# The second MLP's first layer by seven products of quarters, its weights streamed

## The chip, the cores and the metric

One core of a Trainium2 chip runs the kernel, one launch of one program. The engines are TensorE (PE, matrix products; PEld is its weight load), VectorE (DVE), ScalarE (ACT), GpSimd (POOL) and SyncE (SP, which issues most transfers). Each engine works through its own list of instructions in order and waits at semaphores for the others. The metric is the device time of one execution in microseconds; the chip's trace gives each instruction's engine, start and duration.

## What is computed

Attention with decay over q, k, v of 4 batches, 8 heads, 768 positions and 64 columns; its output, 3072 tokens of 512 columns, goes through two MLPs. All values are float32.

```python
# per position t: state = gamma * state + k_t v_t^T ; y_t = scale * q_t state
# first MLP, 512 -> 1024 -> 512
h = x @ w_in;  solu = h * softmax(h);  ln = layernorm(solu) * g_ln;  x = ln @ w_out
# second MLP, 512 -> 2048 -> 512
h = x @ w_in;  g = h * np.cos(h);  out = g @ w_out
```

## The kernel before

Every large product is split: an operand a is kept as a high part (rounded to the type fp32r) and a low part (a minus its high part), and a product is the sum of three matrix products, high·high, low·high and high·low. A "piece" below is three such products of a 128x128 stationary tile with 512 columns, accumulated in a bank of PSUM.

The tokens are worked in 24 steps of 128 and then in 6 blocks of 512. The **first part** (to about 345 us) does attention and the first MLP: per step loads of q, k and v on SyncE, attention, first layer, norm; per block transposes (`transp`, L580, four products into one of two banks tr0 and tr1, from which ScalarE copies the high part and VectorE subtracts the low one) and the second layer (`mm2`), whose result goes to DRAM as y1d. Beside it the weights of the second MLP are unpacked: they are stored as pairs of words that `convert` (L471) puts together, and `keep` (L518) stores them in DRAM.

The **second part** does the second MLP by blocks. `load_y` (L646) loads a block of y1d and splits it into yh and yl. For each of 16 tiles j of 128 hidden columns, `up` (L672) makes the first layer, four pieces of 512 input columns in all (L681), into one of three banks h2, and then the cosine on two engines: ScalarE rounds h/2π to an integer ki (L685), VectorE subtracts ki times 2π in two steps and clamps (L687, L689, L691), ScalarE takes the sine (L693), VectorE multiplies with h (L695), ScalarE copies the high part gh (L697) and VectorE subtracts the low part gl (L699). `down` (L712) multiplies g of a tile with the output weights, four pieces into four banks acc0 to acc3 (L718), three tiles later than `up` (LAG = 3). The weights of this part stay in SBUF, split once into high and low parts by `load_kept` (L752).

A planner sets the order of all this. `P.add` records each operation with its engine, an estimated occupancy and the keys that it reads and writes; at the end `P.order` places the operations one after another by estimated start times and ranks, and emits every engine's list in that order. TensorE's operations may be taken from the next ten of the program's order.

Of the kernel before, what the change touches and what calls it, by code (L numbers as in the profile page):

```python
# [238 lines left out]
def body(ctx: ExitStack, tc: tile.TileContext, qkv, consts,  # L239
# [9 lines left out]
    p_w2a = ctx.enter_context(tc.tile_pool(name="w2a", bufs=1, side="right", reuse_waits="tile"))  # L249
# [221 lines left out]
    def convert(src, use, first=False):  # L471
# [34 lines left out]
    def load_w1(k, c):  # L506
        s = slice(c * 512, (c + 1) * 512)
        convert(w_in1[k * 128:(k + 1) * 128, c * 2048:(c + 1) * 2048],
                (w1h[:, k, s], w1l[:, k, s], ("w1h", k, c), ("w1l", k, c), None), first=(c + k == 0))
# [25 lines left out]
    def mm1(n, c, k, ms=(0, 1, 2)):  # L535
        h, hk = hbank(n, c)
        xh, xl = xhs[n % 2], xls[n % 2]
        s = slice(c * 512, (c + 1) * 512)

        def mm():  # L540
            for m in ms:
                a, w = ((xh, w1h), (xl, w1h), (xh, w1l))[m]
                nc.tensor.matmul(out=h, lhsT=a[:, k], rhs=w[:, k, s], start=(k + m == 0), stop=(k == KD - 1 and m == 2))  # L543
# [77 lines left out]


    def open_sb():
        att.close()
        p2["psh"] = ctx.enter_context(tc.tile_pool(name="psh", bufs=1, side="right", space=PSUM, reuse_waits="tile"))
# [372 lines left out]
```

## Time and profile before

| | us |
|---|---|
| median of 3 runs | 900.62 |
| lowest, highest | 896.74, 902.73 |
| profiled execution | 899.53 |
| its span | 897.7 |
| TensorE busy in it | 873.6 |
| VectorE busy | 571.2 |
| ScalarE busy | 421.5 |

The span runs from the first to the last event of the trace, and the execution's time is measured around it. Busy times of engines overlap. The trace was read as a page (shares of the span, the chain of work that ended last, groups of instructions, transfers) and by queries of stretches and single instructions. "Clock" is the granted clock of TensorE as a share of full speed.

### The profile page before, as it was taken

The numbers are of one execution on the slowest core, as the hardware profiler recorded it, in microseconds if no ns is written. First come the engines' busy times: TensorE is split into PE (matmuls) and PEld (weight loads), VectorE is DVE, ScalarE is ACT, GpSimd is POOL, SyncE is SP. The second block draws the span as 40 slices with busy tenths as digits, with TensorE's granted clock in tenths as the row PEclk, the third lists the DMA queues.
The fourth block names the chain that finished last, engine by engine and source line by source line (L and its number), as shares of the span: only waits on it lengthen the run. The fifth ranks groups of instructions, "written<-read, shape, count | busy, mean of one in ns | idle before, by whom it ended". The sixth has DMA issues, their size and how long they took to land.

```text
span 897.7 us, 14593 instructions
## 1 busy us (share of the span) xinstructions
PE 873.6 (97%) x5888; PEld 722.6 (80%) x5888; DVE 571.2 (64%) x1014; ACT 421.5 (47%) x701; POOL 45.9 (5%) x62
## 2 busy tenths in 40 slices
PE   5998999999999999999999999999999999999997
PEld 4777888888888878888888888888888888888886
DVE  4989858587473665476656565656655565557553
ACT  4688746466452464353343343334433443334332
POOL 2111201011010000000000000000000000000000
PEclk9998999999999999999999999999999999999999
DMA  9993688888520141220020002001200120011002
GB/s 265 295 336 96 189 276 269 296 254 297 161 81 32 50 139 65 82 106 1 24 71 0 1 24 71 0 1 46 49 1 0 48 47 1 1 48 24 1 0 48
DMA packets 38660, 85.17 MB, mean 95 GB/s; under 512 B 5440, under 2 KB 5440, under 8 KB 38592
## 3 DMA queue, kind: packets, MB, share of 16 engines
q1 hardware_dynamic: 38224, 83.24, 29.9%
q10 hardware_dynamic: 368, 0.99, 0.4%
q8 instruction: 46, 0.75, 0.3%
q14 instruction: 22, 0.18, 0.1%
HBM read 64.29 MB, written 19.92 MB: 94 GB/s over the span
## 4 chain that ended last, share of the span: by engine, by line
PE 90%; DMA 4%; DVE 2%; ACT 2%; issue 0%; SPq 0%; ACTq 0%
PE h L681 29%; PE acc L718 29%; PE y L612 12%; PE hA L543 11%; DMA in<-qkv_dram 4%; PE tr L612 2%; PE tr L588 2%; PE y L455 2%; PE sc L390 1%; DMA big<-w_in_dram 1%; ACT junk L321 1%; ACT u L321 0%; DVE in L324 0%; DVE u L332 0%; DVE sm L561 0%; PE S L398 0%
## 5 line engine op out<-in xcount | busy, mean ns | idle before, releaser
L693 ACT ACTIVATE r<-r,hp 128x512 f32<-128x512 f32 x96 | 69.5, 724 | 158.8 <-DVE r L691 158.8
L695 DVE TENSOR_TENSOR r<-r,h 128x512 f32<-128x512 f32 x96 | 66.0, 687 | 65.2 <-ACT r L693 65.2
L612 PE MATMUL y<-lt,o1h 128*128 128x512 f32 x320 | 105.3, 397 | 0.7 <-ACT ys L617 0.7
L687 DVE SCALAR_TENSOR_TENSOR r<-ki,h 128x512 f32<-128x512 int32 x96 | 65.9, 686 | 56.4 <-ACT ki L685 56.4
L699 DVE TENSOR_TENSOR gl<-r,gh 128x512 fp32r<-128x512 f32 x96 | 66.3, 690 | 46.3 <-ACT gh L697 46.3
L718 PE MATMUL acc<-o2u,gh 128*128 128x512 f32 x288 | 94.5, 389 | 0.0
L718 PE MATMUL acc<-o2h,gh 128*128 128x512 f32 x240 | 93.4, 389 | 0.0
L718 PE MATMUL acc<-o2h,gl 128*128 128x512 f32 x240 | 93.4, 389 | 0.0
L718 PE MATMUL acc<-o2l,gh 128*128 128x512 f32 x240 | 93.4, 389 | 0.0
L685 ACT ACTIVATE ki<-h 128x512 int32<-128x512 f32 x96 | 57.4, 598 | 75.1 <-PE h L681 75.1
L697 ACT ACTIVATE gh<-r 128x512 fp32r<-128x512 f32 x96 | 60.5, 630 | 53.0 <-DVE r L695 53.0
L543 PE MATMUL hA<-w1h,xh 128*128 128x512 f32 x176 | 72.2, 410 | 8.9 <-DVE u L332 6.9
L681 PE MATMUL h<-yh,w1h 128*128 128x512 f32 x192 | 74.7, 389 | 0.0
L681 PE MATMUL h<-yh,w1l 128*128 128x512 f32 x192 | 74.7, 389 | 0.0
L681 PE MATMUL h<-yl,w1h 128*128 128x512 f32 x192 | 74.7, 389 | 0.0
L612 PEld LDWEIGHTS y<-lt,o1h 128*128 128x128 f32 x320 | 60.0, 188 | 14.6 <-ACT ys L617 1.2
L543 PE MATMUL hA<-w1h,xl 128*128 128x512 f32 x176 | 69.0, 392 | 0.0
L543 PE MATMUL hA<-w1l,xh 128*128 128x512 f32 x176 | 68.6, 394 | 0.0
L689 DVE SCALAR_TENSOR_TENSOR r<-ki,r 128x512 f32<-128x512 int32 x96 | 66.4, 691 | 3.1
L718 PEld LDWEIGHTS acc<-o2u,gh 128*128 128x128 f32 x288 | 54.0, 188 | 11.2
L612 PE MATMUL y<-lt,o1l 128*128 128x512 f32 x160 | 62.3, 390 | 0.0
L681 PE MATMUL h<-yh,w2a 128*128 128x512 f32 x192 | 59.5, 391 | 0.0
(108 smaller groups left out, 1687.6 us busy)
## 6 DMA issues: line engine op xcount, KB each, us to landing
in<-qkv_dram SPq DMA_DIRECT2D x48, 256.0 KB, 5.1
in<-qkv_dram SPq DMA_DIRECT2D x95, 128.0 KB, 4.7
raw<-w_in_dram SPq DMA_DIRECT2D x16, 511.8 KB, 6.1
raw<-w_out_dram SPq DMA_DIRECT2D x16, 511.8 KB, 4.7
y1d<-ys SPq DMA_DIRECT2D x24, 256.0 KB, 2.5
x<-y1d SPq DMA_DIRECT2D x24, 256.0 KB, 3.1
out_dram<-o SPq DMA_DIRECT2D x48, 128.0 KB, 2.4
kept_out<-wt SPq DMA_DIRECT2D x16, 256.0 KB, 3.6
```

What stands on the lines that cost most here:

```text
L455: nc.tensor.matmul(out=p_y[64 * par:64 * par + 64, j], lhsT=W[par][:, j], rhs=X[par][:, j], start=True, stop=True)
L543: nc.tensor.matmul(out=h, lhsT=a[:, k], rhs=w[:, k, s], start=(k + m == 0), stop=(k == KD - 1 and m == 2))
L612: nc.tensor.matmul(out=y1(), lhsT=w[:, j, ds], rhs=lts[j][:, a], start=(j + m == 0), stop=(j == K1 - 1 and m == 2))
L681: nc.tensor.matmul(out=p2["h2"][b], lhsT=w2tile(c, lo)[:, k, cs], rhs=p2[a][:, k], start=(k + m == 0), stop=(k == KD - 1 and m == 2))
L685: P.add("ACT", 0.5, lambda: nc.scalar.activation(out=p2["ki"][s], in_=p2["h2"][b], func=AF.Identity, scale=INV2PI, bias=0.25), [("h2", b)] ...
L687: P.add("DVE", 0.61, lambda: V.scalar_tensor_tensor(out=p2["r"][s], in0=p2["ki"][s], scalar=-C1, in1=p2["h2"][b], op0=ALU.mult, op1=ALU.ad ...
L689: P.add("DVE", 0.61, lambda: V.scalar_tensor_tensor(out=p2["r"][s], in0=p2["ki"][s], scalar=-C2, in1=p2["r"][s], op0=ALU.mult, op1=ALU.add ...
L693: P.add("ACT", 0.62, lambda: nc.scalar.activation(out=p2["r"][s], in_=p2["r"][s], func=AF.Sin, bias=hp[:, 0:1]), (), [("r", s)])
L695: P.add("DVE", 0.6, lambda: V.tensor_tensor(out=p2["r"][s], in0=p2["r"][s], in1=p2["h2"][b], op=ALU.mult), [("h2", b)], [("r", s)])
L697: P.add("ACT", 0.54, lambda: nc.scalar.activation(out=p2["gh"][g], in_=p2["r"][s], func=AF.Copy), [("r", s)], [("gh", g)])
L699: P.add("DVE", 0.6, lambda: V.tensor_tensor(out=p2["gl"][g], in0=p2["r"][s], in1=p2["gh"][g].bitcast(F32), op=ALU.subtract), [("r", s), (" ...
L718: nc.tensor.matmul(out=p2["acc"][t], lhsT=p2[a][g][:, ts_], rhs=o2tile(j, lo), start=(j == 0 and m == 0), stop=(j == K2 - 1 and m == 2))
```

## The change

Blocks are taken in pairs, and the first layer of a pair is a product of 2x2 quarters: the halves of the 512 input columns, the two blocks of 512 tokens, and the halves of the 2048 hidden columns. Strassen's scheme (in Winograd's form) gives the four quarters of the result from seven products of sums and differences of quarters in place of eight products.

In the first part `prep_w`, `sum_w` and `split_w` make the seven combinations of weights, split them and store them in DRAM (wd, 28 stores of 512 KB), in place of the kept input weights. In the second part `load_w` fetches them tile by tile into a ring of 14 tiles (wr), in the space of the first MLP's weights; `load_x` makes the seven combinations of a pair's tokens. `up` does a "set": seven products of two pieces each into three banks (a: U0 or U3 in turn, b: U1, c: U2), in which products accumulate one on the other; between them ScalarE saves bank a to s, and VectorE adds s and a bank to get h. A set gives two hidden tiles (s and s+8) of both blocks. The even block's g is split and used at once by `down`; the odd block's g is stored to DRAM (gd) and fetched by `fetch_g` in a stretch of 16 `down` behind the pair's eight sets. `merge` puts 14 pieces of `up` and 8 of `down` in turns. All eight tiles of output weights are now loaded in one place (`load_o2`), and the transposes of the last block no longer have first-layer products between them.

```diff
+    def split_w(m, cc, kk, i):
+        n = spl[0] % 2
+        spl[0] += 1
+        st = stages[n]
+        f = wts[i].bitcast(F32).rearrange("p (j c) -> p j c", c=128)
+        act(st[:, :, 0], f, AF.Copy, [("wt", i)], [("st", n, 0)], 0.56)
+        tt(st[:, :, 1], f, st[:, :, 0].bitcast(F32), ALU.subtract, [("wt", i), ("st", n, 0)], [("st", n, 1)], port=True)
+        dma(lambda: nc.sync.dma_start(out=wd[cc][m][:, :, kk].rearrange("j p h c -> p j h c"), in_=st.bitcast(F32)), (512, 1024),
+            [("st", n, 0), ("st", n, 1)], [("wd", cc, m, kk)], occ=0.5)
...
+    def sum_w(o, a, b, op):
+        f = [wts[i].bitcast(F32) for i in (o, a, b)]
+        tt(f[0], f[1], f[2], op, [("wt", a), ("wt", b)], [("wt", o)], port=True)
...
+    def prep_w(cc, kk, step):
+        def piece(mh, kh, i):
+            k, c = kk + 2 * kh, cc + 2 * mh
+            convert(w_in2[k * 128:(k + 1) * 128, c * 2048:(c + 1) * 2048], i)
+        if step == 0:
+            piece(1, 0, 2)
+        if step == 1:
+            piece(1, 1, 3)
+            sum_w(4, 2, 3, ALU.add)
+            split_w(3, cc, kk, 3)
+            split_w(4, cc, kk, 4)
+        if step == 2:
+            piece(0, 0, 0)
+            sum_w(5, 4, 0, ALU.subtract)
+            sum_w(2, 0, 2, ALU.subtract)
+            split_w(0, cc, kk, 0)
+            split_w(5, cc, kk, 5)
+            split_w(6, cc, kk, 2)
+        if step == 3:
+            piece(0, 1, 1)
+            split_w(1, cc, kk, 1)
+            sum_w(1, 1, 5, ALU.subtract)
+            split_w(2, cc, kk, 1)
...
-    def load_y(n):
-        for k in range(KD):
-            b = k % 2
-            dma(lambda k=k, b=b: nc.sync.dma_start(out=x32s[b].rearrange("p a t -> p (a t)"), in_=y1d[n][:, k]), (128, 2048),
-                [("y1d", n, k)], [("x32", b)])
-            P.add("ACT", 0.54, lambda k=k, b=b: nc.scalar.activation(
-                out=p2["yh"][:, k], in_=x32s[b].rearrange("p a t -> p (a t)"), func=AF.Copy),
-                [("x32", b)], [("yh", k)], after=p2["sb_hook"])
-            P.add("DVE", 0.6, lambda k=k, b=b: nc.vector.tensor_tensor(
-                out=p2["yl"][:, k], in0=x32s[b].rearrange("p a t -> p (a t)"), in1=p2["yh"][:, k].bitcast(F32),
-                op=ALU.subtract), [("x32", b), ("yh", k)], [("yl", k)], port=True, after=p2["sb_hook"])
...
+        def part(kk):
+            def sub(o, a, b):
+                f, k = zip(*(half(q) for q in (o, a, b)))
+                tt(f[0], f[1], f[2], ALU.subtract, k[1:], k[:1], port=True)
+
+            def split(m, q):
+                f, k = half(q)
+                P.add("ACT", 0.54, lambda: nc.scalar.activation(out=p2["x"][m][0][:, kk], in_=f, func=AF.Copy),
+                      [k], [("x", m, 0, kk)], after=hook)
+                P.add("DVE", 0.6, lambda: nc.vector.tensor_tensor(
+                    out=p2["x"][m][1][:, kk], in0=f, in1=p2["x"][m][0][:, kk].bitcast(F32), op=ALU.subtract),
...
+            def get(q, n, k):
+                f, key = half(q)
+                dma(lambda: nc.sync.dma_start(out=f, in_=y1d[n][:, k]), (128, 2048), [("y1d", n, k)], [key])
+            get(0, 2 * p, kk)
+            get(1, 2 * p, kk + 2)
+            get(2, 2 * p + 1, kk)
+            get(3, 2 * p + 1, kk + 2)
+            split(0, 0)
+            split(1, 1)
+            sub(4, 2, 0)
+            split(4, 4)
+            sub(5, 3, 4)
+            split(5, 5)
+            sub(1, 1, 5)
+            split(3, 1)
+            sub(2, 3, 2)
+            split(6, 2)
+            split(2, 3)
+        part(0)
+        part(1)
...
+    def products(s):
+        return (0, 1, 5, 4, 6, 3, 2) if s < 7 else (0, 1, 5, 6, 3, 4, 2)
+
+    wn = [0]
+    slot = {}
+
+    def load_w(p, s):
+        for m in products(s):
+            n = wn[0] % NWR
+            wn[0] += 1
+            slot[p, s, m] = n
+            dma(lambda n=n, m=m: nc.sync.dma_start(out=p2["wr"][n].bitcast(F32), in_=wd[s // 4][m][s % 4]), (128, 2048),
+                [("wd", s // 4, m, kk) for kk in (0, 1)], [("wr", n)], after=p2["ring_hook"])
+
+    hn, rn = [0], [0]
...
+              [hk], [("r", r)], port=not bank)
+        if n % 2 == 0:
+            split_g(n, j, lambda: p2["r"][r], ("r", r), j % 2 * 2 + j // 8)
+        else:
+            d = dram.tile([128, 512], F32, name=f"gd{n}_{j}")
+            p2["gd", n, j] = d
+            dma(lambda: nc.sync.dma_start(out=d, in_=p2["r"][r]), (128, 2048), [("r", r)], [("gd", n, j)])
...
+    def fetch_g(n, j, i):
+        b = i % (16 - NWR)
+        dma(lambda: nc.sync.dma_start(out=p2["gs"][b], in_=p2["gd", n, j]), (128, 2048), [("gd", n, j)], [("gs", b)],
+            after=p2["ring_hook"])
+        split_g(n, j, lambda: p2["gs"][b], ("gs", b), i % 4 if i < 10 else 2 + i % 2)
...
+    def up(p, s):
...
+        sets = p * 8 + s
+        a, b, c = 3 * (sets % 2), 1, 2
+        bank = {0: a, 1: b, 4: c, 5: a, 3: a, 6: a, 2: c}
...
+        def save(i):
+            P.add("ACT", 0.5, lambda: nc.scalar.activation(out=p2["s"][i], in_=p2["U"][a], func=AF.Copy), [ka], [("s", i)],
+                  after=p2["cos_hook"])
...
+        def add(n, j, i, u):
+            k = hn[0] % 4
+            hn[0] += 1
+            P.add("DVE", 0.6, lambda: nc.vector.tensor_tensor(out=p2["h"][k], in0=p2["s"][i], in1=p2["U"][u], op=ALU.add),
+                  [("s", i), ("ub", u)], [("h", k)], after=p2["cos_hook"])
+            cosine(n, j, lambda: p2["h"][k], ("h", k))
...
+        def piece(m, kk):
+            u = bank[m]
+
+            def mm():
+                for q, (lo, xl) in enumerate(((0, 0), (1, 0), (0, 1))):
+                    nc.tensor.matmul(out=p2["U"][u], lhsT=p2["wr"][slot[p, s, m]][:, kk, lo], rhs=p2["x"][m][xl][:, kk],
+                                     start=(kk + q == 0 and m in (0, 1, 4)), stop=(kk == 1 and q == 2),
+                                     skip_group_check=True)
+            hook = (*p2["sb_hook"], *p2["ring_hook"], *(p2["wo_hook"] if u == 3 else ()))
+            P.add("PE", 0.68, mm, [("wr", slot[p, s, m]), ("x", m, 0, kk), ("x", m, 1, kk)], [("ub", u)], lat=0.93, after=hook)
+            if kk == 0:
+                return
+            if m == 0:
+                save(0)
+            if m == 1:
+                add(2 * p, s, 0, b)
+            if m == 5:
+                save(1)
+            if m == 6:
+                save(0)
+            if m == (6 if s < 7 else 4):
+                add(2 * p + 1, s + 8, 0, c)
+            if m == 3:
+                cosine(2 * p, s + 8, U(a), ka, True)
+            if m == 2:
+                add(2 * p + 1, s, 1, c)
+        return [lambda m=m, kk=kk: piece(m, kk) for m in products(s) for kk in range(2)]
...
+    p2["ring_hook"] = [P.add("HOOK", 0.0, open_ring, lat=0.0, after=P.using({"w1h", "w1l"}))]
+    load_x(0)
+    load_w(0, 0)
+    load_w(0, 1)
+    for j in range(K1):
+        transp(g, j)
+    p2["cos_hook"] = [P.add("HOOK", 0.0, open_cos, lat=0.0, after=P.using({"u", "x32"}))]
+    mm2(g, 0, None)
+    last = up(0, 0)
+    for d in range(1, 4):
+        mm2(g, d, d % 2)
+        for f in last[(d - 1) * 4:d * 4]:
+            f()
     p2["wo_hook"] = [P.add("HOOK", 0.0, open_wo, lat=0.0, after=P.using({"big", "o1h", "o1l", "xh", "xl", "junk", "ys", "hb"}))]
-    for q in range(2):
...
+    for s in range(4):
+        load_o2(s // 2 if s % 2 == 0 else 4 + s // 2)
+    for s in range(4):
+        load_o2(2 + s // 2 if s % 2 == 0 else 6 + s // 2)
+    for f in last[12:]:
+        f()
+    for p in range(NBLK // 2):
+        for s in range(1, 8):
+            if s < 7:
+                load_w(p, s + 1)
+            a, b = up(p, s), down(2 * p, s - 1, 0) + down(2 * p, s - 1, 1)
+            if s < 7:
+                merge(a, b)
+            else:
+                for f in a[:6] + b[:2] + a[6:8] + b[2:4] + a[8:] + b[4:]:
+                    f()
+        if p + 1 < NBLK // 2:
+            load_x(p + 1)
+            load_w(p + 1, 0)
+            load_w(p + 1, 1)
+        rest = down(2 * p, 7, 0) + down(2 * p, 7, 1)
+        for f in rest:
+            f()
+        for s in range(8):
+            for e in range(2):
+                fetch_g(2 * p + 1, s + 8 * e, 2 * s + e)
+                d = down(2 * p + 1, s, e)
+                if p + 1 < NBLK // 2 and s >= 6:
+                    i = 2 * (s - 6) + e
+                    if i == 0:
+                        nxt_up = up(p + 1, 0)
+                    merge(d, nxt_up[i * 4:i * 4 + 4])
+                else:
+                    for f in d:
+                        f()
```

Three places of the engines' lists. In VectorE's list a set, in the second part. Before, two hidden tiles (L687 and L689 subtract, L691 clamps, L695 multiplies, L699 is the low part):

```order
L695 TENSOR_TENSOR r0_3361<-r0_3361,h20_3354 128x512
L699 TENSOR_TENSOR gl2_3369<-r0_3361,gh2_3365 128x512
L687 SCALAR_TENSOR_TENSOR r1_3362<-ki1_3360,h21_3355 128x512
L689 SCALAR_TENSOR_TENSOR r1_3362<-ki1_3360,r1_3362 128x512
L691 TENSOR_SCALAR r1_3362<-r1_3362 128x512
L695 TENSOR_TENSOR r1_3362<-r1_3362,h21_3355 128x512
L699 TENSOR_TENSOR gl3_3370<-r1_3362,gh3_3366 128x512
```

Now the same operations are L771, L773, L775, L779 and L791, and L818 adds a saved bank and a bank; the first half of a set,

```order
L818 TENSOR_TENSOR hb_3871<-s_3872,U2_3514 128x512
L771 SCALAR_TENSOR_TENSOR ra_3873<-ki_3875,hb_3871 128x512
L773 SCALAR_TENSOR_TENSOR ra_3873<-ki_3875,ra_3873 128x512
L771 SCALAR_TENSOR_TENSOR rb_3874<-ki_3875,U3_4029 128x512
L775 TENSOR_SCALAR ra_3873<-ra_3873 128x512
L773 SCALAR_TENSOR_TENSOR rb_3874<-ki_3875,rb_3874 128x512
L818 TENSOR_TENSOR hb_3871<-s_3872,U2_3514 128x512
L775 TENSOR_SCALAR rb_3874<-rb_3874 128x512
L779 TENSOR_TENSOR ra_3873<-ra_3873,hb_3871 128x512
L771 SCALAR_TENSOR_TENSOR rb_3874<-ki_3875,hb_3871 128x512
L773 SCALAR_TENSOR_TENSOR rb_3874<-ki_3875,rb_3874 128x512
L779 TENSOR_TENSOR rb_3874<-rb_3874,U3_4029 128x512
```

and its second half, after which the next set begins:

```order
L818 TENSOR_TENSOR ha_3870<-s_3872,U1_3513 128x512
L775 TENSOR_SCALAR rb_3874<-rb_3874 128x512
L791 TENSOR_TENSOR gl3_3532<-rb_3874,gh1_3878 128x512
L771 SCALAR_TENSOR_TENSOR ra_3873<-ki_3875,ha_3870 128x512
L779 TENSOR_TENSOR rb_3874<-rb_3874,hb_3871 128x512
L773 SCALAR_TENSOR_TENSOR ra_3873<-ki_3875,ra_3873 128x512
L775 TENSOR_SCALAR ra_3873<-ra_3873 128x512
L779 TENSOR_TENSOR ra_3873<-ra_3873,ha_3870 128x512
L791 TENSOR_TENSOR gl0_3529<-ra_3873,gh_3876 128x512
L818 TENSOR_TENSOR ha_3870<-s_3872,U2_3514 128x512
```

Before, one chain stands behind the other; now four chains and three additions of a set interlace, and the last three operations follow each other's results.

TensorE's list, at the end of a hidden tile's first layer before (L681, then the second layer, L718):

```order
L681 MATMUL h21_3355<-yh_3357,w2h3_3869 128x512
L681 MATMUL h21_3355<-yh_3357,w2l3_3870 128x512
L681 MATMUL h21_3355<-yl_3358,w2h3_3869 128x512
L718 MATMUL acc0_3865<-o2h5_3875,gh3_3366 128x512
L718 MATMUL acc0_3865<-o2h5_3875,gl3_3370 128x512
L718 MATMUL acc0_3865<-o2l5_3876,gh3_3366 128x512
L718 MATMUL acc1_3866<-o2h5_3875,gh3_3366 128x512
```

Now the end of a set (L860 is the second layer, L827 the first; x6, x3, x2 are products 6, 3 and 2 of the seven):

```order
L860 MATMUL acc2_4027<-o2h6_4042,gh_3876 128x512
L860 MATMUL acc2_4027<-o2h6_4042,gl1_3530 128x512
L860 MATMUL acc2_4027<-o2l6_4043,gh_3876 128x512
L860 MATMUL acc3_4028<-o2h6_4042,gh_3876 128x512
L860 MATMUL acc3_4028<-o2h6_4042,gl1_3530 128x512
L860 MATMUL acc3_4028<-o2l6_4043,gh_3876 128x512
L827 MATMUL U3_4029<-x3h_3521,wr12_3702 128x512 x2
L827 MATMUL U3_4029<-x3l_3522,wr12_3702 128x512
L827 MATMUL U3_4029<-x3h_3521,wr12_3702 128x512 x2
L827 MATMUL U3_4029<-x3l_3522,wr12_3702 128x512
L827 MATMUL U2_3514<-x2h_3519,wr13_3703 128x512 x2
L827 MATMUL U2_3514<-x2l_3520,wr13_3703 128x512
```

Before, each tile had a bank of its own; now product 3 accumulates in bank U3, which product 6 finished some pieces earlier and which is saved in between, and product 2 follows at once in U2.

TensorE's list, at the transposes of the last block before (h21 is a bank of the second MLP's first layer):

```order
L681 MATMUL h21_3355<-yl_3358,w2a0_160 128x512
L588 MATMUL tr0_822<-ident_85,u6_100 128x128
L588 MATMUL tr0_822<-ident_85,u0_94 128x128
L588 MATMUL tr0_822<-ident_85,u1_95 128x128
L588 MATMUL tr0_822<-ident_85,u2_96 128x128
L588 MATMUL tr1_823<-ident_85,u6_100 128x128
```

Now (same tiles, new lines):

```order
L636 MATMUL tr1_897<-ident_82,u2_107 128x128
L636 MATMUL tr0_896<-ident_82,u6_111 128x128
L636 MATMUL tr0_896<-ident_82,u0_105 128x128
L636 MATMUL tr0_896<-ident_82,u1_106 128x128
L636 MATMUL tr0_896<-ident_82,u2_107 128x128
L636 MATMUL tr1_897<-ident_82,u6_111 128x128
```

Before, a pair of transposes stood behind a first-layer tile; now tr0 and tr1 come again right behind their first use, four transposes in a row.

## Rows read from the trace of the kernel before

**Rows 1.** The page, part 1: busy us, share of the span, instructions.
```profile
PE 873.6 (97%) x5888; PEld 722.6 (80%) x5888; DVE 571.2 (64%) x1014; ACT 421.5 (47%) x701; POOL 45.9 (5%) x62
```

**Rows 2.** The page, part 4: the chain that ended last, by engine.
```profile
PE 90%; DMA 4%; DVE 2%; ACT 2%; issue 0%; SPq 0%; ACTq 0%
```

**Rows 3.** The chain's pieces in order of time: start, us, what.
```profile
457.20 10.88 PE h L681 x48
```

**Rows 4.** Stretches: bounds, length, busy us (count) by engine, clock, DMA share, GB/s.
```profile
50.00:100.00 50.00, 44.98 (x605) 37.13 (x605) 47.84 (x96) 44.69 (x80) 10.33 (x10) 0.93 0.58 188
100.00:150.00 50.00, 50.00 (x428) 41.26 (x430) 34.72 (x74) 27.90 (x47) 6.76 (x9) 1.00 0.81 265
150.00:200.00 50.00, 50.00 (x564) 41.66 (x554) 35.96 (x75) 28.74 (x48) 5.55 (x7) 1.00 0.85 276
200.00:250.00 50.00, 50.00 (x490) 41.50 (x490) 31.98 (x69) 26.14 (x46) 6.49 (x8) 1.00 0.66 214
```

**Rows 5.** Timeline 600 to 612 us: start, us, engine, line, operation [idle before, releaser].
```profile
603.92 0.39 PE L718 MATMUL acc<-o2h,gh 128*128 128x512 f32 x1
...
604.18 0.60 ACT L685 ACTIVATE ki<-h 128x512 int32<-128x512 f32 x1 [0.79 <-PE h L681]
...
604.81 0.69 DVE L687 SCALAR_TENSOR_TENSOR r<-ki,h 128x512 f32<-128x512 int32 x1 [0.69 <-ACT ki L685]
...
605.53 0.69 DVE L689 SCALAR_TENSOR_TENSOR r<-ki,r 128x512 f32<-128x512 int32 x1
...
606.26 0.43 DVE L691 TENSOR_SCALAR r<-r 128x512 f32<-128x512 f32 x1
...
606.72 0.72 ACT L693 ACTIVATE r<-r,hp 128x512 f32<-128x512 f32 x1 [1.94 <-DVE r L691]
...
607.48 0.69 DVE L695 TENSOR_TENSOR r<-r,h 128x512 f32<-128x512 f32 x1 [0.79 <-ACT r L693]
...
608.20 0.63 ACT L697 ACTIVATE gh<-r 128x512 fp32r<-128x512 f32 x1 [0.76 <-DVE r L695]
...
608.87 0.69 DVE L699 TENSOR_TENSOR gl<-r,gh 128x512 fp32r<-128x512 f32 x1 [0.70 <-ACT gh L697]
```

**Rows 6.** Timeline of VectorE, 360 to 368 us, a dense stretch.
```profile
363.74 0.42 DVE L691 TENSOR_SCALAR r<-r 128x512 f32<-128x512 f32 x1
364.07 0.68 DVE L687 SCALAR_TENSOR_TENSOR r<-ki,h 128x512 f32<-128x512 int32 x1
364.79 0.69 DVE L689 SCALAR_TENSOR_TENSOR r<-ki,r 128x512 f32<-128x512 int32 x1
365.40 0.68 DVE L695 TENSOR_TENSOR r<-r,h 128x512 f32<-128x512 f32 x1
365.99 0.42 DVE L691 TENSOR_SCALAR r<-r 128x512 f32<-128x512 f32 x1
```

**Rows 7.** Groups by line and form: line, operation, count, busy us, mean ns, idle before.
```profile
L324 DVE TENSOR_TENSOR x<-y,mg 128x512 f32<-128x512 f32 x24 | 16.6, 690 | 0.5
...
L617 ACT ACTIVATE ys<-y 128x512 f32<-128x512 f32 x20 | 11.9, 596 | 38.4 <-PE y L612 26.9 <-DMA y1d<-ys 7.3 <-issue 3.1
...
L760 DVE TENSOR_TENSOR o2l<-raw,o2h 128x1024 fp32r<-128x1024 f32 x5 | 6.0, 1222 | 13.5 <-ACT o2h L759 13.5
...
L759 ACT ACTIVATE o2h<-raw 128x1024 fp32r<-128x1024 f32 x5 | 5.2, 1050 | 0.0
```

**Rows 8.** The page, part 6: transfers of 256 KB, us from issue to landing.
```profile
x<-y1d SPq DMA_DIRECT2D x24, 256.0 KB, 3.1
```

**Rows 9.** Stretches of 10 us, columns as in rows 4.
```profile
60.00:70.00 10.00, 5.53 (x111) 4.48 (x109) 9.85 (x24) 9.45 (x16) 2.59 (x3) 0.91 1.04 330
70.00:80.00 10.00, 9.45 (x40) 7.80 (x40) 9.26 (x15) 8.28 (x16) 1.42 (x1) 0.75 0.08 23
320.00:330.00 10.00, 9.26 (x41) 7.35 (x40) 5.59 (x12) 7.71 (x10) 0.55 (x1) 1.00 0.37 112
```

**Rows 10.** Timeline of TensorE, 320 to 324 us: a product behind a wait.
```profile
322.49 0.50 PE L612 MATMUL y<-lt,o1h 128*128 128x512 f32 x1 [0.74 <-ACT ys L617]
```

More of the change, by code (lines that the diff above doesn't have):

```diff
@@ L537, in mm1 @@
         xh, xl = xhs[n % 2], xls[n % 2]
-        s = slice(c * 512, (c + 1) * 512)
         def mm():
             for m in ms:
-                a, w = ((xh, w1h), (xl, w1h), (xh, w1l))[m]
-                nc.tensor.matmul(out=h, lhsT=a[:, k], rhs=w[:, k, s], start=(k + m == 0), stop=(k == KD - 1 and m == 2))
+                a, lo = ((xh, 0), (xl, 0), (xh, 1))[m]
+                nc.tensor.matmul(out=h, lhsT=a[:, k], rhs=w1[lo][k][c], start=(k + m == 0), stop=(k == KD - 1 and m == 2))
         r = [("xh", n % 2)]
@@ L703, in o2tile, with half @@
-    def o2tile(j, lo):
-        g = j // 2
-        if g < UBUF // 2:
-            return o2u[2 * g + lo][:, j % 2]
-        return p2["o2"][g][lo][:, j % 2]
-    def o2key(g, lo):
-        return [("u", 2 * g + lo, c) for c in (0, 1)] if g < UBUF // 2 else [("o2", g, lo)]
-    def down(n, j, tiles=range(4)):
-        g = p2["g", n, j]
-        for t in tiles:
-            def mm(t=t):
+    def half(q):
+        return raws[q // 2][:, (q % 2) * 512:(q % 2 + 1) * 512].bitcast(F32), ("raw", q // 2, q % 2)
@@ L755, in load_kept, with merge @@
         t = raws[n % NRAW].bitcast(F32).rearrange("p (e f) -> p e f", e=2)
-        rk = ("raw", n % NRAW)
-        d = kept[what]
-        dma(lambda: nc.sync.dma_start(out=t, in_=d), (128, 4096), [("kept",) + what + (k,) for k in (0, 1)], [rk])
-        P.add("ACT", 0.95, lambda: nc.scalar.activation(out=tile_of(0), in_=t, func=AF.Copy), [rk], hk, after=after)
-        P.add("DVE", 1.14, lambda: nc.vector.tensor_tensor(out=tile_of(1), in0=t, in1=tile_of(0).bitcast(F32),
-                                                           op=ALU.subtract), [rk] + hk, lk, port=True, after=after)
+        rk = [("raw", n % NRAW, h) for h in (0, 1)]
+        d = kept[g]
+        dma(lambda: nc.sync.dma_start(out=t, in_=d), (128, 4096), [("kept", g, k) for k in (0, 1)], rk)
+        P.add("ACT", 0.95, lambda: nc.scalar.activation(out=p2["o2"][g][0], in_=t, func=AF.Copy), rk, [("o2", g, 0)],
+              after=p2["wo_hook"])
+        P.add("DVE", 1.14, lambda: nc.vector.tensor_tensor(out=p2["o2"][g][1], in0=t, in1=p2["o2"][g][0].bitcast(F32),
+                                                           op=ALU.subtract), rk + [("o2", g, 0)], [("o2", g, 1)], port=True,
+              after=p2["wo_hook"])
+    def merge(a, b):
+        n, m = len(a), len(b)
+        i = j = 0
+        while i < n or j < m:
+            if j >= m or (i < n and i * m <= j * n):
+                a[i]()
+                i += 1
+            else:
+                b[j]()
+                j += 1
     loaded = [0]
@@ L805, in attend @@
         if n == ns - 1:
-            p2["sb_hook"] = [P.add("HOOK", 0.0, open_sb, lat=0.0, after=P.using({"in", "amg", "sc", "S", "y"}))]
+            p2["sb_hook"] = [P.add("HOOK", 0.0, open_sb, lat=0.0, after=P.using({"in", "amg", "sc", "S", "y", "wt", "st", "top"}))]
     def first(n, c):
```

199 lines of the change are left out of this document (78 added, 121 removed).

## The prediction

> **What bounds the kernel now.** I read the page's busy shares first: TensorE is busy for 873.6 of 897.7 us, VectorE for 64%, ScalarE for 47% [rows 1]. A share this high makes TensorE's work the first suspect, and the chain that ended last confirms it: 90% of it is TensorE, transfers and the other engines share the rest [rows 2]. The chain's pieces then tell at which rate that work runs: 48 products of the second MLP's first layer take 10.88 us [rows 3], so a product of 512 columns costs 10.88/48 = 0.2267 us and a piece of three 0.68 us. The stretches show where it is not so: from 50 to 100 us TensorE loses 5.0 us of 50, VectorE being busy for 47.84 there; from 100 us on it is busy throughout at clock 1.00, with VectorE at 32 to 36 of 50 [rows 4]. So a product that goes away in the second part is worth 0.2267 us, as long as VectorE, ScalarE and the banks keep up at the shorter pace. That is the question of this case, since the change pays for its products in VectorE, ScalarE and transfers.
>
> My sum is made against the profiled execution, 899.53 us (897.7 of span and 1.83 around it); the median of the runs is 900.62, 0.12% above.
>
> **Products removed.** Seven products of quarters in place of eight: the first layer goes from 1152 to 1008 products, the second stays at 1152, the rest of TensorE's list keeps its numbers. 144 x 0.2267 = 32.6 us less. Nothing covers TensorE there, so all of it counts if no new wait comes: 866.9 us.
>
> **A set of four hidden tiles.** A set is 14 pieces of the first layer with 8 pieces of the second between them: 22 x 0.68 = 14.96 us of TensorE. Its other side is VectorE: three additions of a saved bank to a bank, four cosine chains of four operations, two low parts, 17 long operations and 4 clamps (the order rows of VectorE). Two views price them. In the ordinary run of the kernel before, a chain shows each operation and each trip to ScalarE: 0.69 us an operation, 0.43 the clamp, and waits of 0.69, 0.79 and 0.70 us for ScalarE's three steps [rows 5]. In a dense stretch the operations start closer than they last: those at 364.79, 365.40 and 365.99 start 0.61 and 0.59 apart, one that needs the result just before it 0.72, and after a clamp the next starts 0.33 later [rows 6]. With the starts of the dense stretch, 17 x 0.60 + 4 x 0.34 = 11.6; the order leaves three trips to ScalarE uncovered (behind the addition of U2, and behind the last clamp and the last multiplication of the set), each the operation's time and the wait less the start already counted: 0.69 + 0.69 - 0.60, 0.43 + 0.79 - 0.34 and 0.69 + 0.70 - 0.60, together 2.45; four starts behind their own result add 0.12 each, 0.5. Sum 14.5 us, below 14.96: TensorE still sets the pace, with 0.5 us to spare. I take this value, because the rows with the short starts are VectorE's own under load. The other end has no overlap at all: 17 x 0.69 + 4 x 0.43 = 13.45, plus the waits of 0.69, 0.79 and 0.70, is 15.63 us.
>
> The Trainium skill ("VectorE: DVE Perf Modes", section "Terms") has a rule that speaks for that other end: each operation is followed by a flush, and the next can't issue until the pipe is empty. By it the sets would be paced by VectorE; the starts 0.6 us apart of operations that last 0.68 or 0.69 [rows 6] speak against it, and the measurement decides.
>
> **ScalarE.** A set has three saves, four first steps, four sines, two copies of high parts: 7 x 0.60 + 4 x 0.72 + 2 x 0.63 = 8.3 us of 14.96 [rows 5, 7]; free, apart from its place in the waits.
>
> **Waits for banks.** The tightest point of TensorE in a set is product 3: it starts at 18 x 0.68 = 12.24 us and overwrites nothing, but accumulates into the bank that must first be saved after product 6, which ends at 16 x 0.68 = 10.88. From the last piece to ScalarE's start the trace shows 0.26 us (603.92 to 604.18), a copy out of a bank takes 0.60 [rows 5, 7]: free at 11.74, 0.5 us early. Product 2 at 13.60 needs the addition of U2, of 0.69 us, behind that save: about 12.5, 1.1 us early. A queue on ScalarE of one operation eats the first margin now and then: between 0 and 18 x 0.3 = 5 us, I take 1.
>
> **Streaming.** A tight set fetches seven weight tiles and stores two tiles of g, 9 x 256 KB in 14.96 us, 158 GB/s; the trace moved 276 GB/s from 150 to 200 us [rows 4], and the ring holds two sets, so a transfer of 3.1 us [rows 8] has a set's time. Free; without that cover the price is the transfer, once per set. The fetches of the odd block have 5.44 us per round of two buffers against 3.1 + 0.60 + 0.69 = 4.4: free too.
>
> **The turn from the first part to the second.** Eight transposes used to have first-layer products of the second MLP between them; now four stand in a row over two banks (the order rows of the transposes). Each bank is copied (0.26 + 0.60) and subtracted (0.69) before it is free [rows 5, 7], so the third waits some 1.2 us and the fourth 0.2: +1.4. Afterwards pieces of the first MLP's second layer lie between.
>
> **The first sets.** Eight tiles of output weights are split there, 1.05 us on ScalarE and 1.22 on VectorE each [rows 7]; some of the eight were split in the same place before, beside a VectorE with more room. Against 0.5 us of room per set, 8 x 1.22 = 9.8 us has to be fitted into the looser first set: 0 to 5 us, I take 2.
>
> **Preparation in the first part.** 16 sums, and 28 splits for 4, are 40 more long operations on VectorE, 40 x 0.69 = 27.6 us [rows 7], mostly between 100 and 250 us, where it is busy for 34.72 + 35.96 + 31.98 = 102.7 of 150 [rows 4]; 130.3 is 87%. At 69% TensorE loses nothing, at 96% (50 to 100) 5 of 50, though cold start and loads share that blame. Between them lie 0 and about 10 us; no product waits for a prepared weight until the second part, so I take 2.5. The stores of prepared weights, 28 x 512 KB, stand in SyncE's order later than the loads that TensorE waits for; the transfer share of 0.81 to 0.85 [rows 4] is why I don't take 0.
>
> Sum: 866.9 + 1 + 1.4 + 2 + 2.5 = 873.8, **874 us**.
>
> **Rivals.**
> *VectorE paces the sets* (15.63 for 14.96): 18 tight sets (6 in each of 3 pairs) x 0.67 = 12 us, 886. For: three new additions and uncovered trips. Against: [rows 6]. Chance 0.14.
>
> *The preparation delays the first part* by its upper bound, 10 us instead of 2.5 (rounded with a transfer or two that comes late), 884. For: VectorE at 96% with TensorE losing 10% [rows 4]. Against: preparation has no early reader. Chance 0.12. Both together, 896: chance 0.08, no measurable change.
>
> *The clock falls*, the case that ends slower. TensorE now meets a bank just saved at product 3 in each set; if short waits there take the granted clock to its lower level, 1.2 for 2.4 GHz, products cost twice as much while it lasts. If a quarter of the tight sets run so, 18/4 x 14.96 = 67 us come on top, 941; with 36 us of TensorE's work at the low level it ends above 909.6, so that point is 2.4 sets. For: after 60 to 70 us, in which TensorE worked for 5.53 of 10, the clock of the next 10 us was 0.75 [rows 9]. Against: a wait of 0.74 us at 322 us [rows 10] is in a stretch with clock 1.00 [rows 9], and the waits priced above are shorter. Chance 0.08. The Trainium skill ("TensorE: Matmul & The Clock Gate", section "A second HAM failure mode: psum-queue depth-cycling") describes such a kernel, whose short idle times between groups at bank changes made the clock swing; the single wait in [rows 10] does not bear it out.
>
> **How the numbers follow.** Forecast (TensorE paces, small terms between their ends: 866 to 880) 0.54, the rivals 0.14, 0.12, 0.08 and 0.08; 0.04 remains for what I have not seen, half below, half about no change. The low end is 866, where every added cost is nothing; the high end 892 takes in both single rivals with some room: 0.54 + 0.14 + 0.12 = 0.80. One per cent of 900.62 is about what a measurement tells from no change: faster below 891.6, slower above 909.6. Faster: 0.54 + 0.14 + 0.12 + 0.02 = 0.82; within 1%: 0.08 + 0.02 = 0.10; slower 0.08.
>
> **What would show it.** Right: TensorE's busy time down by some 33 us, pieces of the first layer with no idle time before them longer than some tenths, the period of a set 15.0 us, granted clock 1.00 throughout, the second part starting within 5 us of before. VectorE at nearly no idle time with 15.6 us per set would show the first rival; TensorE idle before 250 us, or a second part that starts 10 us late, the second; stretches with a clock below 1.00 after 100 us the third. Wrong is the forecast too if weights land late: idle time of TensorE before a first-layer piece put down to a transfer.

## The result, and the profile after

The changed kernel took 874.73 us (median) against 901.24; the ratio is 0.9702, 95% interval 0.9673 to 0.9732: 3% faster, where 874 was forecast. Three of the four runs took 871.64 to 876.93 us; the fourth had a mean granted clock of 0.608 (1306.77 us), so the profile read here is that of another execution of the same kernel (874.92 us, span 873.1). The page's shares [rows 1] and chain [rows 2] are now:

```profile
PE 844.3 (97%) x5744; PEld 696.9 (80%) x5744; DVE 633.7 (73%) x1148; ACT 482.3 (55%) x823; POOL 51.5 (6%) x62
```
```profile
PE 83%; DVE 7%; DMA 6%; ACT 3%; issue 1%; SPq 0%; ACTq 0%; DVEq 0%
```

TensorE is still busy for 97%; 144 products and 29.3 us of its busy time are gone, and VectorE gained 62 us. The products of the second MLP's first layer alone, each counted to the start of the next, took 261.6 us before and 228.5 now. In stretches (columns as in [rows 4]), the three between 100 and 250 us, and four sets of the first pair, each exactly one TensorE period long:

```profile
100.00:150.00 50.00, 50.00 (x442) 41.52 (x432) 42.57 (x83) 33.73 (x60) 7.75 (x9) 1.00 0.92 297
150.00:200.00 50.00, 50.00 (x571) 41.12 (x570) 42.65 (x80) 33.25 (x59) 6.43 (x7) 1.00 0.90 289
200.00:250.00 50.00, 50.00 (x495) 41.59 (x494) 36.35 (x81) 30.02 (x52) 7.27 (x8) 1.00 0.89 282
...
395.40:410.36 14.96, 14.96 (x67) 12.39 (x67) 14.89 (x26) 9.99 (x17) 0.00 (x0) 1.00 0.80 260
410.36:425.32 14.96, 14.96 (x67) 12.39 (x67) 14.96 (x26) 8.23 (x14) 0.00 (x0) 1.00 0.74 230
440.28:455.24 14.96, 14.96 (x67) 12.39 (x67) 12.43 (x22) 8.22 (x13) 0.00 (x0) 1.00 0.55 155
455.24:470.20 14.96, 14.96 (x67) 12.39 (x67) 12.18 (x22) 8.00 (x13) 0.00 (x0) 1.00 0.53 162
```

The period is 14.96 us, the product of 22 pieces, in every tight set. In a clean set VectorE is busy for 12.2 to 12.4 us; in those that also split output weights for up to 14.96 of 14.96, and TensorE does not wait even there. VectorE's own waits stand at the end of a clean set:

```profile
465.79 0.43 DVE L775 TENSOR_SCALAR ra<-ra 128x512 f32<-128x512 f32 x1
467.00 0.69 DVE L779 TENSOR_TENSOR ra<-ra,hb 128x512 f32<-128x512 f32 x1 [0.79 <-ACT ra L777]
468.39 0.69 DVE L791 TENSOR_TENSOR gl<-ra,gh 128x512 fp32r<-128x512 f32 x1 [0.70 <-ACT gh L789]
469.57 0.69 DVE L818 TENSOR_TENSOR hb<-s,U 128x512 f32<-128x512 f32 x1 [0.48 <-ACT s L812]
470.95 0.69 DVE L771 SCALAR_TENSOR_TENSOR ra<-ki,hb 128x512 f32<-128x512 int32 x1 [0.70 <-ACT ki L769]
```

Three of them are trips to ScalarE and back; the one of 0.48 us is for the save of a bank, which hangs on TensorE. What TensorE waited for from 300 us on (engine, line, releaser: us, times, longest):

```profile
PE y L660 <- ACT ys L665: 1.1, 1, 1.1
PE acc L860 <- DVE gl L791: 1.1, 3, 0.5
PE tr L636 <- DVE lt L647: 1.0, 1, 1.0
PE acc L860 <- ACT gh L789: 0.6, 1, 0.6
```

The single instructions behind them, and the bank that product 3 needs:

```profile
348.76 1.26 PE L636 MATMUL tr<-ident,u 128*128 128x128 f32 x8 [0.97 <-DVE lt L647]
...
468.45 0.39 PE L827 MATMUL U<-x6l,wr 128*128 128x512 f32 x1
...
468.94 0.60 ACT L812 ACTIVATE s<-U 128x512 f32<-128x512 f32 x1 [0.58 <-PE U L827]
...
470.04 0.61 PE L827 MATMUL U<-x3h,wr 128*128 128x512 f32 x2
...
819.21 0.49 PE L860 MATMUL acc<-o2h,gh 128*128 128x512 f32 x1 [0.55 <-ACT gh L789]
820.08 0.50 PE L860 MATMUL acc<-o2h,gl 128*128 128x512 f32 x1 [0.38 <-DVE gl L791]
```

Product 6's last product begins at 468.45, the save ends at 469.54, product 3 starts at 470.04: the 0.5 us of margin that was worked out, and no wait. The transposes wait as foreseen. The waits at 819 us were not foreseen: the last tile of the even block, needed behind the eight sets, comes out of its cosine chain too late, at the end of each pair's sets.

The chain's pieces at the same two places of the first part, before and after:

```profile
98.82 5.67 PE hA L543 x24
...
324.14 5.46 PE hA L543 x24
```
```profile
100.60 5.67 PE hA L591 x24
...
325.82 5.45 PE hA L591 x24
```

225.32 us before, 225.22 now: the preparation of the weights, nearly all of which lies between (26 of its 28 stores), cost nothing. The 1.8 us by which this profile starts later are there before VectorE's and ScalarE's lists first differ (an operation at 88.77 us before is at 90.55 now), and the twelve traces of changed kernels have anything from 98.7 to 102.4 us at this place.

### The profile page after: what moved, and what is told of

Read it like the earlier page. It is cut to its first block, busy times and chain, and to the rows that moved or that the text cites. A ratio compares the mean times of both kernels' runs of the same rounds, so it can differ in the third digit from the quotient of the medians.

```text
span 1305.0 us, 15238 instructions
## 1 busy us (share of the span) xinstructions
PE 1287.3 (99%) x5744; PEld 809.7 (62%) x5744; DVE 646.4 (50%) x1148; ACT 489.1 (37%) x823; POOL 49.9 (4%) x62
## 4 chain that ended last, share of the span: by engine, by line
PE 98%; DMA 1%; DVE 0%; issue 0%; ACT 0%; SPq 0%
PE acc L860 29%; PE U L827 26%; PE hA L591 16%; PE y L660 14%; PE tr L636 3%; PE tr L660 3%; PE y L456 3%; PE sc L391 2%; PE hB L591 1%; PE S L399 1%; DMA in<-qkv_dram 1%; PE sc L392 0%; DVE u L333 0%; DVE in L325 0%; SPq L350 0%
## 5 line engine op out<-in xcount | busy, mean ns | idle before, releaser
L860 PE MATMUL acc<-o2l,gh 128*128 128x512 f32 x384 | 196.7, 512 | 0.0
L860 PE MATMUL acc<-o2h,gl 128*128 128x512 f32 x384 | 196.4, 511 | 0.0
L860 PE MATMUL acc<-o2h,gh 128*128 128x512 f32 x384 | 196.3, 511 | 0.0
L660 PE MATMUL y<-lt,o1h 128*128 128x512 f32 x320 | 159.7, 578 | 0.7 <-ACT ys L665 0.7
L860 PEld LDWEIGHTS acc<-o2l,gh 128*128 128x128 f32 x384 | 79.9, 208 | 47.0 <-issue 17.0
L860 PEld LDWEIGHTS acc<-o2h,gl 128*128 128x128 f32 x384 | 79.3, 207 | 47.3 <-issue 17.2
L860 PEld LDWEIGHTS acc<-o2h,gh 128*128 128x128 f32 x384 | 79.5, 207 | 46.8 <-issue 15.8
L812 ACT ACTIVATE s<-U 128x512 f32<-128x512 f32 x72 | 43.1, 598 | 147.4 <-PE U L827 147.2
L791 DVE TENSOR_TENSOR gl<-gs,gh 128x512 fp32r<-128x512 f32 x48 | 33.2, 691 | 112.9 <-ACT gh L789 112.7
L818 DVE TENSOR_TENSOR ha<-s,U 128x512 f32<-128x512 f32 x36 | 24.7, 686 | 82.5 <-PE U L827 41.3
L591 PEld LDWEIGHTS hA<-w1l,xh 128*128 128x128 f32 x176 | 38.6, 220 | 27.7 <-issue 15.7
L818 DVE TENSOR_TENSOR hb<-s,U 128x512 f32<-128x512 f32 x36 | 24.7, 686 | 62.4 <-ACT s L812 36.4
L591 PEld LDWEIGHTS hA<-w1h,xh 128*128 128x128 f32 x176 | 37.9, 215 | 27.9 <-issue 15.9
```

The costliest lines, as they stand in the source:

```text
L591: nc.tensor.matmul(out=h, lhsT=a[:, k], rhs=w1[lo][k][c], start=(k + m == 0), stop=(k == KD - 1 and m == 2))
L660: nc.tensor.matmul(out=y1(), lhsT=w[:, j, ds], rhs=lts[j][:, a], start=(j + m == 0), stop=(j == K1 - 1 and m == 2))
L791: P.add("DVE", 0.6, lambda: nc.vector.tensor_tensor(out=p2["gl"][g], in0=src(), in1=p2["gh"][g].bitcast(F32), op=ALU.subtract), [key, ("gh ...
L812: P.add("ACT", 0.5, lambda: nc.scalar.activation(out=p2["s"][i], in_=p2["U"][a], func=AF.Copy), [ka], [("s", i)], after=p2["cos_hook"])
L818: P.add("DVE", 0.6, lambda: nc.vector.tensor_tensor(out=p2["h"][k], in0=p2["s"][i], in1=p2["U"][u], op=ALU.add), [("s", i), ("ub", u)], [( ...
L860: nc.tensor.matmul(out=p2["acc"][t], lhsT=p2[a][g][:, ts_], rhs=p2["o2"][j // 2][lo][:, j % 2], start=(j == 0 and m == 0), stop=(j == K2 - ...
```

## The experiments

Effects are against the changed kernel. The first four ran together. The next four have the kernel before at 900.75 us, to which 0.969 of `again` makes 872.8 for the changed kernel.

**again**: the changed kernel, unaltered.

> The changed kernel once more, unaltered, for a profile at full clock. By the forecast: 874 us, granted clock 1.00 from 100 us on, a tight set takes 15.0 us, TensorE's idle time before products 3 and 2 is a few tenths at most, and the second part starts within 5 us of the kernel before. VectorE as the pace of the sets: a period of 15.6 us with VectorE nearly never idle. Preparation late: the second part starts some 10 us late.

873.86 us, ratio 0.969 (0.9668 to 0.9712). The marks of the forecast stand in the rows above: 14.96 us for a tight set, clock 1.00 from 100 us on, no wait before products 3 and 2, and the place shortly before the second part is reached 1.7 us later than before (325.82 for 324.14).

**no_clamp**

```diff
-        P.add("DVE", 0.35, lambda: V.tensor_scalar(out=p2["r"][r], in0=p2["r"][r], scalar1=HI, scalar2=LO,
-                                                   op0=ALU.min, op1=ALU.max), (), [("r", r)], port=True)
```

> The clamp of the cosine is left out (96 operations on VectorE of 0.43 us, four in a set); its result is the same for arguments that need no clamp. Forecast, TensorE paces the sets: a set falls on VectorE's side from 14.5 to about 13.1 us, TensorE's 14.96 stay; the time changes by 0 to -3 us against the changed kernel (the -3 from the first sets). VectorE paces the sets: 18 tight sets times 0.67 us, -12 us.

871.97 us (869.68 to 873.22), -1.9, which is within the spread of the runs. 1.4 us less of VectorE in each set did not shorten the sets, which still take 14.96: TensorE paces them.

**add_twice**

```diff
+            P.add("DVE", 0.6, lambda: nc.vector.tensor_tensor(out=p2["h"][k], in0=p2["s"][i], in1=p2["U"][u], op=ALU.add),
+                  [("s", i), ("ub", u)], [("h", k)], after=p2["cos_hook"])
```

> Each addition of a saved bank and a bank is done twice (72 more operations of 0.69 us on VectorE, three in a set). With 0.5 us to spare on VectorE, a set goes from 14.5 to 14.5 + 3 x 0.6 = 16.3 us, 1.3 above TensorE's 14.96: 18 x 1.3 = +24 us against the changed kernel. If VectorE paces the sets already: 18 x 1.8 = +32 us. If it has more room than worked out, 2 us or more: 0 to +5 us.

872.83 us (868.95 to 873.4): no cost. Neither my sum (+24) nor the rival (+32) holds; VectorE had at least 1.8 us more to give in a set. The sets of the second and third pair still start 14.96 us apart. One of them in the columns of [rows 4], and the end of a later set on VectorE:

```profile
574.00:588.96 14.96, 14.96 (x68) 12.39 (x67) 13.89 (x25) 7.73 (x14) 0.00 (x0) 1.00 0.51 167
```
```profile
616.42 0.43 DVE L775 TENSOR_SCALAR ra<-ra 128x512 f32<-128x512 f32 x1
616.76 0.68 DVE L779 TENSOR_TENSOR rb<-rb,hb 128x512 f32<-128x512 f32 x1
617.64 0.69 DVE L779 TENSOR_TENSOR ra<-ra,hb 128x512 f32<-128x512 f32 x1 [0.19 <-ACT ra L777]
```

The planner made another order: behind the clamp, where the changed kernel waits 0.79 us for ScalarE's sine, another multiplication now stands. My sum had added the three operations to the old order with its trips open.

**no_stream**

```diff
+            if wn[0] > NWR:
+                continue
             dma(lambda n=n, m=m: nc.sync.dma_start(out=p2["wr"][n].bitcast(F32), in_=wd[s // 4][m][s % 4]), (128, 2048),
```

> The 154 later loads of the ring are left out: every set computes with the 14 weight tiles loaded first. Forecast, the stream is hidden: 0 to -1 us against the changed kernel. If late weights or a shared transfer path hold TensorE or the fetches of the odd blocks: -3 us or more.

874.44 us (872.81 to 875.02): nothing gained. From 590 to 640 us the transfer share falls from 0.54 to 0.09 and TensorE is busy for 50.00 of 50 in both: the stream is hidden.

**add_four**: the two added lines of add_twice three times.

> Each addition of a saved bank and a bank is done four times: 9 more long operations of VectorE in a set, 26 long ones and 4 clamps. If starts of 0.60 us set VectorE's pace and trips to ScalarE hide behind other work: 26 x 0.60 + 4 x 0.34 = 17.0 us a set, 2.0 above TensorE's 14.96, 18 x 2.0 = +37 us against the changed kernel. If the trips stay uncovered as in the prediction's sum (2.9 us more a set): +89 us. If each operation costs its whole duration: 26 x 0.69 + 4 x 0.43 + 2.2 = 21.9, +125 us.

937.68 us, ratio 1.0403 (1.0382 to 1.0425), +65. Here VectorE is the pace (busy for 17.14 us from 625.30 to 642.60). The last sets of the second and third pair are 17.3 us apart: starts of 0.60 (17.0) explain that, whole durations (19.7, and 21.9 with trips) don't. None of the three totals came. Counted at the starts of product 5 against `again`, the first pair's sets, which also split output weights, are 22 us longer in sum (up to 21.7 us each), those of the second and third pair 8 and 9, and the three stretches behind them, where the backlog is paid, 8 to 10 each. The clock has a part in this: behind five waits it was at 0.50, for 20.5 us in all. One of these waits, and the clock around it (1-us stretches):

```profile
438.90 0.39 PE L833 MATMUL U<-x1l,wr 128*128 128x512 f32 x1
441.94 1.22 PE L833 MATMUL U<-x2h,wr 128*128 128x512 f32 x2 [2.65 <-DVE hb L824]
```
```profile
440.00:441.00 1.00, 0.00 (x0) 0.00 (x0) 1.00 (x3) 0.53 (x1) 0.00 (x0) 1.00 0.95 340
...
442.00:443.00 1.00, 1.00 (x3) 0.81 (x4) 1.00 (x3) 0.53 (x2) 0.00 (x0) 0.50 0.95 356
...
446.00:447.00 1.00, 1.00 (x6) 0.82 (x5) 1.00 (x3) 0.00 (x0) 0.00 (x0) 1.00 0.89 227
```

After 2.65 us without work the clock was at its lower level for some 3 us; the two products at 441.94 show 1.22 us for the 0.61 of the row at 470.04.

**no_p3**

```diff
+            if m != 3:
+                P.add("PE", 0.68, mm, [("wr", slot[p, s, m]), ("x", m, 0, kk), ("x", m, 1, kk)], [("ub", u)], lat=0.93, after=hook)
```

> Product 3 of the seven is left out on TensorE (144 products; the loads and all work of the other engines stay). VectorE with 2.5 us or more of room in a set: TensorE's 13.6 us set the pace, 144 x 0.2267 = -32.6 us against the changed kernel. VectorE with the 0.5 us of the prediction's sum: 18 tight sets give 0.5 each and 6 loose ones 1.36 each, -17 us. VectorE at its whole durations: about 0 to -8.

841.53 us, ratio 0.9345 (0.9317 to 0.9374), -31. The sets come 13.60 us apart, 20 pieces: a product is worth its 0.2267 us even one step further. VectorE follows, again in another order of the planner, with 12.10 us of work in a set:

```profile
602.78:616.38 13.60, 13.60 (x61) 11.26 (x60) 12.10 (x21) 8.01 (x14) 0.00 (x0) 1.00 0.56 174
```

**p0_twice**

```diff
+            for _ in range(2 if m == 0 else 1):
+                P.add("PE", 0.68, mm, [("wr", slot[p, s, m]), ("x", m, 0, kk), ("x", m, 1, kk)], [("ub", u)], lat=0.93, after=hook)
```

> Product 0 is done twice, so that a set has eight products again (its second piece then counts twice in the result); everything else of the change stays. If the additions, the stream, the stores and fetches and the preparation cost nothing: 144 x 0.2267 = +32.6 us against the changed kernel, some 5 us above the kernel before, which is then what all the rest of the change costs. If the rest costs 10 us or more: above 911.

907.2 us, ratio 1.007 (1.0053 to 1.0086), +34: with eight products a set the sets are 16.32 us apart, and all that the change adds costs 6 us over the kernel before.

**p3_close**

```diff
-                    for k, i in enumerate(pe[:self.WINDOW]):
+                    for k, i in enumerate(pe[:1 if pe and pe[0] >= self.cut else self.WINDOW]):
...
+    P.cut = len(P.ops)
...
-                merge(a, b)
+                merge(a[:8], b)
+                for f in a[8:]:
+                    f()
```

> From the second set on TensorE keeps the program's order, and in sets 1 to 6 products 6, 3 and 2 stand directly behind one another, so that product 3 waits for the save of its bank in each of 18 sets: 0.26 + 0.60 + some 0.07 = 0.93 us each. If the clock holds: 18 x 0.93 = +17 us against the changed kernel, granted clock 1.00. If short waits at banks in every set lower the clock (the prediction's slower case): stretches at 0.5 in the sets, +60 us and more.

901.61 us, ratio 1.0007 (0.9994 to 1.0021), +29; the whole gain is gone by the order of pieces alone. The wait is there in each set, and the clock holds:

```profile
603.48 0.39 PE L828 MATMUL U<-x6l,wr 128*128 128x512 f32 x1
604.61 0.73 PE L828 MATMUL U<-x3h,wr 128*128 128x512 f32 x2 [0.75 <-ACT s L813]
```
```profile
440.00:450.00 10.00, 9.25 (x41) 7.16 (x40) 6.42 (x11) 4.93 (x8) 0.00 (x0) 1.00 0.48 154
```

Sets are 16.13 us apart, 1.17 more and not 0.93: 18 x 1.17 = 21, where the spans of the two profiles differ by 26.8 (899.9 and 873.1). Of the rest, 3.9 us are waits for additions at four other places, which the strict order brought, and 1.8 us are four waits of the second layer for a tile of g in the first pair, three of whose sets are 18.4, 17.1 and 16.6 us long; since the changed kernel's own waits at the ends of the sets (1.7 us) are gone, a few us stay open.

**v1** and **v2**: three small waits taken away, by the pieces between the transposes, the order of a pair's last set (kept as written on TensorE), and the order of the last three tiles, whose pieces are collected in `late` (the last block's tiles of g also take turns in all four buffers). The core of v1:

```diff
+    last[0]()
+    last[2]()
+    transp(g, 2)
+    transp(g, 3)
+    mm2(g, 0, None, range(2))
...
-                for f in a[:6] + b[:2] + a[6:8] + b[2:4] + a[8:] + b[4:]:
+                for f in a[:6] + b[:2] + a[6:8] + b[2:4] + a[8:10] + b[4:] + a[10:]:
...
+    for t in range(4):
+        for d in late:
+            d[t]()
```

v2 differs from v1 in one line:

```diff
-                for f in a[:6] + b[:2] + a[6:8] + b[2:4] + a[8:10] + b[4:] + a[10:]:
+                for f in a[:6] + b[:2] + a[6:8] + b[2:4] + a[8:12] + b[4:] + a[12:]:
```

> The changed kernel with three small waits taken away: two first-layer pieces and the first pieces of the first MLP's last product stand between the transposes (1.2 us); in the last set of a pair all pieces of the second layer but four stand behind product 3, so that the even block's last tile has 8.2 us instead of 6.8 for its chain (2.5 us over three pairs); the last three tiles are finished bank by bank, so that the output stores don't leave together (1.4 us). If these waits are what the profile shows them to be: -4 to -5 us against the changed kernel. If each only moves to the next point: 0 to -1.5.

> The changed kernel unaltered, beside v1 on the same chip: 873 to 875 us.

v1 took 874.1 us (872.4 to 875.49), the changed kernel beside it 873.8: nothing gained. The waits at the ends of the pairs' sets and at the last stores were gone; at the transposes a wait of 0.74 us for ScalarE's copy of a bank of y had come in place of the 0.97; and product 2 now came too soon behind product 4 into the same bank:

```profile
PE U L828 <- DVE hb L819: 2.9, 3, 1.3
```

> As v1, but in the last set of a pair product 4 stands directly behind product 3, the second layer's pieces behind it and product 2 last, so that product 2 no longer follows product 4 into bank U2 while its addition is still to come (v1's new wait, 2.9 us over three pairs). The transposes' wait stays away, the stores leave in turn. If that was all that ate v1's gain: 4 us below the changed kernel, 870. If the waits only move again: 873 to 874.

> The changed kernel unaltered, beside v2 on the same chip: 873 to 875 us.

v2 took 868.53 us, ratio 0.9646 (0.9625 to 0.9667), and the changed kernel beside it 872.95 (0.9687): -4.4, in size as expected. From 325 us on TensorE has one wait left, the new one between the transposes (that of [rows 10] stands earlier, at 323.74 us):

```profile
PE y L661 <- ACT ys L666: 0.7, 1, 0.7
```
```profile
349.70 0.50 PE L661 MATMUL y<-lt,o1h 128*128 128x512 f32 x1 [0.74 <-ACT ys L666]
```

So of the three waits that of the transposes only moved, and the turn became 0.3 us shorter. The gain lies in the other two: the second layer's products take 260.9 us in sum for 264.1, and from TensorE's last product to the end of the span it is 5.1 us for 7.1.

The end shows the third of the waits: eight output stores leave together in the changed kernel, spread in v2 (SyncE's queue, start and us):

```profile
865.29 4.96 SPq L872 DMA_DIRECT2D out_dram<-o  x8
```
```profile
856.75 7.22 SPq L873 DMA_DIRECT2D out_dram<-o  x8
```

## Why the prediction was right

**The main term** was right, in place and size: 144 x 0.2267 = 32.6 us. no_p3 (-31) and p0_twice (+34) measure the same price on both sides of the change, and the sets take 14.96 us. TensorE's whole busy time fell by 29.3 us, where some 33 were named as a sign; 1.6 us of the difference lie ahead of the second part, up to the first of the two places above (80.72 us busy before, 82.33 now).

**Who paces the sets** was right, and so was VectorE's sum, for the order that the changed kernel has. The three trips that were foreseen stand open in its clean sets, 0.79, 0.70 and 0.70 us; beside 12.2 us of busy time and pauses of some hundredths they leave the 0.48 us in which VectorE waits for the save. 14.96 - 0.48 = 14.5, the value foreseen, and the margin is the 0.5 us of the sum. What failed is what I drew from that margin, for the first sets and in the expectations of add_twice and no_p3: it belongs to one order and is not the room for other work. Where VectorE had more to do, the planner put it into the trips: VectorE is busy for 14.96 of 14.96 us in a set that splits output weights, and for 13.89 in add_twice. So the 2 us for the first sets were 0. The starts of 0.60 and 0.34 us hold at full load too (17.3 for 17.0 in add_four).

**Product 3's bank**: margin 0.5 us as worked out (469.54 to 470.04), cost 0 instead of 1. p3_close shows what the order is worth where it is missing.

**The stream and the fetches**: free, as said. **The preparation**: 0 us instead of 2.5, with VectorE at 85% from 100 to 200 us and a transfer share of 0.90 to 0.92; the share of 50 to 100 us was no guide, since the loss there is one single wait, in both kernels (5.0 us before, 5.1 now):

```profile
PE hA L543 <- DVE u L332: 5.0, 1, 5.0
```

**The transposes**: 1.0 us of wait and 1.2 in sum, for 1.4.

**Not foreseen**: the end of a pair's sets. The second layer's products, each counted to the start of the next, took 264.1 us in sum for 260.9 before, and 3.1 of the 3.2 us lie behind the three pairs' sets, at 490, 654 and 819 us, where the even block's last tile comes late. And the tail: from TensorE's last product (892.01 and 866.04) to the end of the span 5.7 us before and 7.1 now, 1.4 more.

So the small terms came to 1.2 + 3.2 + 1.4 us and 0.4 at the wait of [rows 10], now 1.1 us: 6.2, where 1 + 1.4 + 2 + 2.5 = 6.9 were foreseen (with the 1.8 us of this execution's later start, 32.6 - 8.0 = 24.6 us, the difference of the spans): the forecast of 874 was met this closely by luck, because terms that I had too high stood against two that I did not have. p0_twice, 6 us above the kernel before, has about the same sum of costs.

**The rivals.** VectorE as the pace is refuted (no_clamp, add_twice). The rule of the Trainium skill ("VectorE: DVE Perf Modes", section "Terms"), that the next operation can't issue until the pipe is empty, does not agree with sets of 17.3 us for 26 long operations and 4 clamps in add_four, whose durations alone are 19.7. The preparation did not delay the first part. The clock did not fall: the longest wait here from 300 us on is 1.13 us, and 18 waits of up to 0.75 us left it at 1.00 in p3_close, while five of 2.0 to 3.1 us were followed by 0.50 in add_four. The Trainium skill ("TensorE: Matmul & The Clock Gate", section "A second HAM failure mode: psum-queue depth-cycling") is not borne out by the short waits at banks of p3_close, only by the longer ones of add_four.

## What to carry to other kernels

Where TensorE runs without waits, a product removed is worth its full time as long as the list of the busiest other engine, starts and not durations, with the trips to other engines that nothing fills, fits into the shorter period. The margin of one order is not the room for more work: where operations were added, the planner's new order put them into the open trips. Look then at the seams, where one schedule gives way to another and at the last stores: here nearly all of the change's own cost lay there, and 4.4 us of it could be taken back by moving pieces. After such a move look at what each moved piece now stands directly behind, since v1 lost at a bank what it had gained.

## What the runs showed of the hardware

A wait of TensorE costs more than its length when the clock falls behind it: after 2.65 us at 441.94 the granted clock was 0.50, its lower level, for some 3 us (six products took 2.73 us, for 1.36). The length of the wait alone does not decide this. In add_four the clock fell at waits of 1.99, 2.65, 2.65, 2.91 and 3.09 us (at 461, 421, 442, 692 and 874 us) and stayed at 1.00 at others of 1.80, 2.10 and 2.91 us (at 409, 480 and 512 us); in p3_close, with 0.75 us in every set and single waits of up to 1.18, it stayed at 1.00 in all of them.

A short stop also costs more than the wait that is printed: sets with a wait of 0.75 us were 1.17 us longer. Most of it can be read from starts. The product in front of the wait starts at 603.48 and product 3 at 604.61, 1.14 us later for the usual 0.23, so 0.91 us are lost: the 0.75 are counted from the end of a record of 0.39 us, and the next product would have started 0.16 before that end. The two products behind the wait show 0.73 us for 0.61, another 0.12. The rest, about 0.13, is a second, shorter stop in front of product 5, between two of the second layer's products (0.30 us between their starts at 597.68, and again one set later).
